# ScalarE's share of the gV blocks, and the pace of the weight gradients, in a decode block's forward and backward pass

## The chip, the cores and the metric

The kernel runs on one core of a Trainium2 chip. The metric is the device time of one execution in microseconds (us). The profile is one execution, taken by the hardware profiler. Engines: PE (TensorE), VectorE (DVE in the profile), ScalarE (ACT), GpSimd (POOL) and the issuing queue SyncE (SP). Each works off its own instructions in the order in which the program holds them.

## The reference

One decode step of a transformer block (2 sequences, 32 heads of 128, 4096 cached keys, width 640, all bfloat16) and its gradients by every input but one:

```python
h = x + A_ref(layernorm(x), k_cache, v_cache, wq, wo)   # scores, softmax, p @ v, then @ wo
h2 = h + B_ref(layernorm(h), w1, w2)                    # relu MLP, hidden width 1728
# returned: h2, and the gradients of x, k_cache, v_cache, wq, wo, w1, w2 for grad_out
```

For the attention the two large gradients are outer products, for each batch b and head h: the gradient of V is `p` (4096) times `go` (128), and that of K is `p * (go.v - dot) * scale` (4096) times `q` (128). Each is a 1 MB tensor, and there are 64 of either kind. The gradients of the four weight matrices are outer products too, of rank 2 (one term for each sequence).

## The kernel before

Each cached tile of 4096 x 128 lies in SBUF as [128, 32, 128]: 32 blocks (`NSC`) of 128 rows.

**First pass** (`p1_iter`, one head each): K is transposed on PE, the scores and the softmax are made, the products that later steps need are kept. Its 66 steps go over both batches.

**Second pass** (`p2_iter(j)` and `p2_tail(j)`, one turn j for each of 64 heads in the order `turns`): V comes in again (tile `W`, loaded on SyncE's queue; 12 of the 64 are kept from the first pass). PE transposes it in four groups (`pair_transpose`, L435; ScalarE copies each group out of PSUM, L440), and multiplies it by `go` (`pair_matvec`, L448). `rb` (L872, ScalarE) holds the rows `go` and `q` spread over all partitions; `pp` (L874, GpSimd) holds p, each value twice. Then VectorE makes the gradient of V, `gV`, in two halves of 16 blocks (`outer_half`, L832), and GpSimd's queue stores it (L900). In the next turn `p2_tail` makes `gsp` (L843) and from it the gradient of K, `gK`, in two halves on VectorE (L832), stored at L851. gV and gK take buffers of the group "g", five and later seven of them, W those of "ld", the weight gradients those of "f".

With `by_act`, ScalarE makes the last 8 blocks (`NSB`) of gV instead of VectorE, each as one copy of the row scaled by a column of `pf` (L899); `pf` is a float copy by GpSimd (L877). VectorE's second half is then 8 blocks instead of 16. Before the change this holds for the turns 14 to 31: those after the end of the first pass and below 32.

**Order.** A list `plan` pairs the steps of the first pass with turns of the second: from step 41 on every other step has a turn, and from turn 14 on there are turns alone. A turn is a Python generator; after each of its seven parts the loop calls `bg_step` for three queues of background work. Each queue earns a `rate` of credit for a part and takes the next piece when it has some. Queue 0 is the middle of the network and the `go` rows (`go_group`, VectorE dot products at L658). Queue 1 is `fin_gen`, the weight gradients: `rows_of` prepares rows (L913, L918, L920), `outer_rows` makes 152 outer products on PE (L950), copies each by ScalarE to a tile `ot` (L956), and stores it with 19 transfers issued on ScalarE's queue (L959). Queue 2 is `gx_gen`, the gradient of x (dot products at L658). Queues 1 and 2 begin when the pool `fin` is made, during turn 23; their rates are `RATE2` and `RATE3`.

The outcome of all this is one fixed order of instructions for each engine; nothing is decided on the chip.

Of the kernel before, what the change touches and what calls it, by code (L numbers as in the profile page):

```python
# [10 lines left out]
ACT = mybir.ActivationFunctionType  # L11
# [4 lines left out]
def kernel(  # L16
# [20 lines left out]
    nc = tc.nc  # L37

    B, Sq, D = A_x.shape
    _, H, Sk, Dh = A_k_cache.shape  # L40
# [4 lines left out]
    NSC = Sk // 128  # L45
# [7 lines left out]
    HALF = NSC // 2  # L53
# [153 lines left out]
    P_bf = cols.tile([128, NPS, NSC], BF16)  # L207
# [194 lines left out]
    NP1 = len(pairs)  # L402
# [6 lines left out]
    p_slot = {bh: n for n, bh in enumerate(pairs[:NPS])}  # L409
# [417 lines left out]
    def pairs_view(t):  # L827
        return t.rearrange("p s (a two) -> p s a two", two=2)

    def outer_half(dst, row, colp, k, n=HALF):  # L830
        sl = slice(k * HALF, k * HALF + n)
        nc.vector.tensor_tensor(  # L832
            out=pairs_view(dst[:, sl, :]),
            in0=row.rearrange("p (a two) -> p a two", two=2)[:, None, :, :].to_broadcast([128, n, 64, 2]),
            in1=colp[:, sl, None, :].to_broadcast([128, n, 64, 2]), op=ALU.mult)

    def p2_tail(j):

        p = S2[j]
        bp, hp = turns[j]  # L840
        pair_matvec(p["dp"], p.pop("T3"), 3, gom[:, bp, hp, :, :])
        gsp = small.tile([128, NSC, 2], BF16, tag="gsp", bufs=2, name="gsp")
        nc.vector.scalar_tensor_tensor(  # L843
            out=gsp[:], in0=p["dp"][:, :, None].to_broadcast([128, NSC, 2]), scalar=negdot[:, hp, bp:bp + 1],
            in1=P_bf[:, p_slot[(bp, hp)], :, None].to_broadcast([128, NSC, 2]), op0=ALU.add, op1=ALU.mult)
        yield
        gK = take("g", [128, NSC, 128], "gK")
        outer_half(gK, p["rb"][:, 128:256], gsp, 0)
        yield
        outer_half(gK, p["rb"][:, 128:256], gsp, 1)  # L850
        nc.gpsimd.dma_start(out=natural(out_2, bp, hp), in_=gK[:])  # L851
        give(gK)
        del S2[j]
        yield

    NSB = 8

    def p2_iter(j, by_act):

        tail = p2_tail(j - 1) if j - 1 in S2 and "T3" in S2[j - 1] else iter(())  # L860
        c = S2[j]
        next(tail, None)
        b, h = turns[j]
        go = gom[:, b, h, :, :]
        bank = pst([128, 512], FP32, "sps", "dp_ps")
        for k, col in enumerate((goc, qsc)):
            nc.tensor.matmul(bank[:, 128 + k * 128:256 + k * 128],  # L867
                             lhsT=col[:, h, b:b + 1].to_broadcast([128, 128]), rhs=ident_bf[:],
                             start=True, stop=True)
        c["dp"] = bank[:, 0:NSC]  # L870
        rb = mats.tile([128, 256], BF16, tag="rb", bufs=3, name="rb")
        nc.scalar.activation(out=rb[:], in_=bank[:, 128:384], func=ACT.Copy, scale=rt[:, b, h:h + 1])  # L872
        pp = small.tile([128, NSC, 2], BF16, tag="pp", bufs=2, name="pp")
        nc.gpsimd.tensor_copy(out=pp[:], in_=P_bf[:, p_slot[(b, h)], :, None].to_broadcast([128, NSC, 2]))  # L874
        if by_act:
            pf = small.tile([128, NSB], FP32, tag="pf", bufs=2, name="pf")
            nc.gpsimd.tensor_copy(out=pf[:], in_=P_bf[:, p_slot[(b, h)], NSC - NSB:NSC])  # L877
        c.update(rb=rb, pp=pp)
        c["T0"] = pair_transpose(c["W"], 0)
        next(tail, None)  # L880
        yield
        for _ in tail:
            yield
        c["T1"] = pair_transpose(c["W"], 1)
        pair_matvec(c["dp"], c.pop("T0"), 0, go)
        yield
        c["T2"] = pair_transpose(c["W"], 2)
        pair_matvec(c["dp"], c.pop("T1"), 1, go)
        yield
        c["T3"] = pair_transpose(c["W"], 3)  # L890
        give(c["W"], "g" if j < H and j != 1 and owned["g"] < 3 else None)
        pair_matvec(c["dp"], c.pop("T2"), 2, go)
        gV = take("g", [128, NSC, 128], "gV")
        outer_half(gV, c["rb"][:, 0:128], c["pp"], 0)
        yield
        outer_half(gV, c["rb"][:, 0:128], c["pp"], 1, HALF - NSB if by_act else HALF)
        if by_act:
            for k in range(NSB):
                nc.scalar.activation(out=gV[:, NSC - NSB + k, :], in_=rb[:, 0:128], func=ACT.Copy, scale=pf[:, k:k + 1])  # L899
        nc.gpsimd.dma_start(out=natural(out_3, b, h), in_=gV[:])  # L900
        give(gV)
        yield
# [190 lines left out]
    M0_ITERS = 7  # L1093
    P2_AT = H + 2 + M0_ITERS
    RATES = (0.2, 0.8, 0.2, 0.8, 0.45)
    RATE2 = 0.65
    RATE3 = 0.45
    plan = []
    i = j = 0
# [46 lines left out]
    fin = big1 = big2 = big3 = None  # L1146
    g2 = None
# [12 lines left out]
    for n, (i, j) in enumerate(plan):  # L1160
        all_go = all(("go", B - 1, h) in done for h in range(H))
        if i is None and plan[n - 1][0] is not None:
            pkp.release()
            big1 = tc.alloc_tile_pool(name="big1", bufs=1)
            for _ in range(2):
                more_home("ld", big1)
            share(ld=KEPT[1] + 4, g=5)
        if all_go and not late[0]:
            wop.release()
            big3 = tc.alloc_tile_pool(name="big3", bufs=1, side="right")  # L1170
            for tag in ("ld", "g", "g", "q", "q", "q"):
                more_home(tag, big3)
        late[0] = all_go
        more = int(late[0])
        if fin is not None and not bg2 and not bg3:
            share(ld=8 + 3 * more, g=7 + 3 * more)
        elif fin is not None and j >= H:
            held = sum(bh in kept for bh in turns[j + 1:])
            share(ld=5 + held + more, g=5 + 2 * more, f=3, q=2 + 3 * more)
        while g2 is not None:  # L1180
            p2_step()
        open_tail = [k for k in S2 if "T3" in S2[k]]
        if j is not None:
            if j < NP1:
                bg_until(("go", *turns[j]))
            g2 = p2_iter(j, i is None and j < H) if j < NP1 else p2_tail(NP1 - 1)
        elif open_tail:
            g2 = p2_tail(open_tail[0])
        if i is None and ("w1", 1) in done and fin is None:
            wts.release()  # L1190
            fin = tc.alloc_tile_pool(name="fin", bufs=1)
            big2 = tc.alloc_tile_pool(name="big2", bufs=1)
            more_home("f", big2)
            banks.update(sps=[2, 3], o=[4, 5, 6])
            bg2.append(("fin", fin_gen(fin)))
            bg3.append(("gx", gx_gen(fin)))
        if i == 12:
            bg.append(("ga", ga_gen()))
        if i == H + 2:
            banks["bc"].insert(0, banks["sps"].pop(0))  # L1200
        elif i == P2_AT:
            banks["bc"].remove(7)
            banks["sps"].insert(0, banks["bc"][0])
            banks["bc"] = [7]
        rate = RATES[0 if i is not None and i <= H + 1 else 1 if j is None and i < P2_AT else
                     2 if i is not None else 3 if j <= H else 4]
        if i is None:
            spread[0] = 2
            at_k[0] = 1
            k = 0  # L1210
            while g2 is not None:
                p2_step()
                pump()
                slot[0] = int(k in ((1, 3, 5) if j <= H else (1, 4)))
                k += 1
                bg_step(0, rate)
                bg_step(1, RATE2 * (0.4 if spreading[0] else 1.0))
                bg_step(2, RATE3)
            continue
        at = LIGHT if j is None else HEAVY_TAIL if open_tail else HEAVY  # L1220
        for k, _ in enumerate(p1_iter(i, i < H + 1, 0)):
            for _ in range(at.get(k, 0)):
                if g2 is not None:
                    p2_step()
            if k == 5:
                a_heads(i)
            pump()

            spread[0] = 1 if i < P2_AT else 2
            at_k[0] = k  # L1230
            if i >= P2_AT:
                slot[0] = int(k == 6 or (k == 1 and j is None))
            elif i > H + 1:
                slot[0] = {1: 2, 3: 1, 4: 1, 6: 1}.get(k, 0)
            else:
                slot[0] = int(k in (1, 6))
            bg_step(0, rate)
            bg_step(1, 0.0)
        if i is not None and i in (H + 1, NP1 + 1):
            bg.append((f"m{i // H - 1}", middle_gen(i // H - 1)))  # L1240
# [41 lines left out]
```

## Time and profile before

| | us |
|---|---|
| median of 3 runs (lowest, highest) | 897.04 (895.9, 898.17) |
| the profiled execution | 896.38 |
| its span, first to last instruction | 894.5 |
| busy: PE / VectorE / ScalarE / GpSimd | 744.0 / 684.9 / 483.4 / 196.1 |
| bytes moved | 361.84 MB, 405 GB/s in the mean |

In the profile a line such as `L899 ACT ACTIVATE gV<-rb,pf x144` names the line of the kernel, the engine, the operation, what is written from what, and the count. "DMA share" is the mean busy share of the 16 DMA engines. PEclk is the granted clock of TensorE as a share of full speed; its mean is 0.768, and in the second pass it is mostly 0.5.

### The profile page before, as it was taken

The page shows a single profiled execution, that of the slowest core. Times are in us where ns is not written, and L with a number is a line of the kernel's source. Part 1 is how long each engine was busy: PE and PEld are TensorE (multiplying, and loading weights), DVE is VectorE, ACT ScalarE, POOL GpSimd, SP SyncE. Part 2 cuts the span into 40 slices and gives each one's busy share as a digit, 9 for nine tenths or more (in the row PEclk, how much of TensorE's full clock was granted, in tenths as well). Part 3 has the DMA queues.
Part 4 walks back from the last instruction along what each step waited for, and adds up shares of the span by engine and source line. Part 5 has one row for each costly group of instructions (what it writes and reads, how often), then busy time and mean ns, then how long its engine had stood idle before and what let it go on. Part 6 is the DMA issues. An engine that isn't in the chain of part 4 may idle for free.

```text
span 894.5 us, 24705 instructions
## 1 busy us (share of the span) xinstructions
PE 744.0 (83%) x10145; PEld 619.9 (69%) x10145; DVE 684.9 (77%) x1283; ACT 483.4 (54%) x1236; POOL 196.1 (22%) x347
## 2 busy tenths in 40 slices
PE   4998899998998998798768786788798897988593
PEld 4887788888787887787657675567566665664453
DVE  2665788966888897697678896679886679978854
ACT  1443344443555665465446777776665765656462
POOL 1344434442210000000011231122221111111211
PEclk9999999999999999899895555555755756555555
DMA  9999999999989999999999999999999999999996
GB/s 376 419 411 404 409 407 419 410 414 410 364 299 374 421 423 424 424 420 424 406 374 399 416 418 421 385 417 389 421 421 411 422 425 425 425 425 426 423 407 271
DMA packets 56304, 361.84 MB, mean 405 GB/s; under 512 B 5696, under 2 KB 11904, under 8 KB 15488
## 3 DMA queue, kind: packets, MB, share of 16 engines
q1 hardware_dynamic: 34536, 211.13, 58.0%
q0 software_dynamic: 18432, 134.23, 36.1%
q10 hardware_dynamic: 3224, 14.92, 4.2%
q8 instruction: 80, 1.31, 0.6%
q14 instruction: 32, 0.26, 0.1%
HBM read 211.11 MB, written 149.13 MB: 403 GB/s over the span
## 4 chain that ended last, share of the span: by engine, by line
PE 40%; DMA 28%; DVE 17%; ACT 7%; issue 5%; SPq 0%; POOL 0%; ACTq 0%; POOLq 0%; DVEq 0%
PE t_ps L435 17%; DMA Vt<-in_A_v_cache_dram 12%; DMA out_dram<-gK 9%; PE m_ps L469 8%; DMA out_dram<-gV 5%; DVE gK L832 4%; DVE rows L658 4%; PE s_ps L448 3%; DVE gV L832 3%; DVE pk L476 3%; PE o_ps L950 3%; PE dp_ps L448 2%; ACT gV L899 2%; ACT t_sb L440 2%; PE u_ps L498 2%
## 5 line engine op out<-in xcount | busy, mean ns | idle before, releaser
L440 ACT COPY t_sb<-t_ps 128x512 f32<-128x512 f32 x479 | 271.9, 586 | 188.0 <-PE t_ps L435 184.5
L448 PEld LDWEIGHTS <-t_sb 128*128 128x128 bf16 x4096 | 169.8, 103 | 87.9 <-issue 39.8
L435 PE MATMUL t_ps<-ident_f,Wt 128*128 128x128 f32 x832 | 203.8, 398 | 0.7 <-ACT t_sb L440 0.7
L476 DVE TENSOR_TENSOR pk<-Kt,ep 128x2048 bf16<-128x2048 bf16 x128 | 156.2, 1221 | 42.5 <-ACT ep L523 23.4
L469 PE MATMUL m_ps<-pk,Vt 128*128 128x129 bf16 x2048 | 174.7, 223 | 16.7 <-DMA Vt<-in_A_v_cache_dram 15.4
L832 DVE TENSOR_TENSOR gK<-rb,gsp 128x2048 bf16<-128x2048 bf16 x128 | 153.0, 1223 | 15.1 <-DMA out_dram<-gV 13.3
L435 PEld LDWEIGHTS t_ps<-ident_f,Wt 128*128 128x128 f32 x832 | 142.4, 207 | 31.6 <-issue 23.6
L435 PE MATMUL t_ps<-ident_f,Kt 128*128 128x128 f32 x1024 | 149.7, 281 | 6.1 <-DMA Kt<-in_A_k_cache_dram 5.6
L832 DVE TENSOR_TENSOR gV<-rb,pp 128x2048 bf16<-128x2048 bf16 (+1 forms) x128 | 143.4, 1144 | 10.0 <-DMA out_dram<-gK 9.1
L469 PEld LDWEIGHTS <-Vt 128*128 128x128 bf16 x2048 | 129.9, 99 | 20.3 <-DMA Vt<-in_A_v_cache_dram 18.3
L435 PEld LDWEIGHTS t_ps<-ident_f,Kt 128*128 128x128 f32 x1024 | 113.3, 145 | 7.6 <-issue 4.9
L486 POOL COPY pk<-ep 128x16 bf16<-128x16 bf16 x80 | 83.0, 1039 | 151.6 <-ACT ep L523 111.9
L448 PE MATMUL dp_ps<-gom,t_sb 128*128 128x2 bf16 x2048 | 96.4, 168 | 19.0 <-ACT t_sb L440 18.5
L900 POOL DMA_DIRECT2D out_dram<-gV x64 | 34.2, 534 | 312.6 <-DVE nb L516 115.1
L448 PE MATMUL s_ps<-gom,t_sb 128*128 128x2 bf16 x2048 | 79.9, 164 | 1.5 <-DVE t_sb L438 1.5
L851 POOL DMA_DIRECT2D out_dram<-gK x64 | 34.0, 531 | 215.1 <-DVE gK L832 166.5
L582 ACT CAST MT<-m_ps 128x128 bf16<-128x128 f32 x64 | 17.0, 265 | 115.8 <-PE m_ps L469 115.8
L956 ACT CAST ot<-o_ps 128x512 bf16<-128x512 f32 (+3 forms) x152 | 67.6, 492 | 3.5 <-PE o_ps L950 1.9
L872 ACT ACTIVATE rb<-dp_ps,rt 128x256 bf16<-128x256 f32 x64 | 30.2, 471 | 42.4 <-PE dp_ps L867 41.2
L658 DVE CUSTOM_DVE_ANT_0 rows<-wo_t,rows 128x640 bf16<-128x640 bf16 x64 | 52.5, 820 | 0.2
L843 DVE SCALAR_TENSOR_TENSOR gsp<-dp_ps,negdot,P_bf 128x64 bf16<-128x64 f32 x64 | 17.9, 279 | 43.7 <-PE dp_ps L448 43.4
L658 DVE CUSTOM_DVE_ANT_0 rows<-wqs,gqr 128x1024 bf16<-128x1024 bf16 x40 | 48.8, 1219 | 0.2
(194 smaller groups left out, 759.5 us busy)
## 6 DMA issues: line engine op xcount, KB each, us to landing
Kt<-in_A_k_cache_dram SPq DMA_DIRECT2D x64, 1024.0 KB, 16.8
Vt<-in_A_v_cache_dram SPq DMA_DIRECT2D x64, 1024.0 KB, 17.0
out_dram<-gV POOLq DMA_DIRECT2D x64, 1024.0 KB, 12.2
out_dram<-gK POOLq DMA_DIRECT2D x64, 1024.0 KB, 12.9
Wt<-in_A_v_cache_dram SPq DMA_DIRECT2D x52, 1024.0 KB, 12.8
out_dram<-ot ACTq DMA_DIRECT2D x6, 960.0 KB, 8.6
wq_t<-in_A_wq_dram SPq DMA_DIRECT2D x5, 1024.0 KB, 7.0
wqs<-in_A_wq_dram SPq DMA_DIRECT2D x5, 1024.0 KB, 21.9
```

The lines of the kernel that those rows point to most:

```text
L435: nc.tensor.transpose(t_ps[:, j, :], natf[:, 2 * cc:2 * cc + 2, :].rearrange("p c k -> p (c k)"), ident_f[:])
L440: nc.scalar.copy(out=t_sb[:], in_=t_ps[:])
L448: nc.tensor.matmul(dst[:, sc:sc + 2], lhsT=v[:, j, :, par], rhs=vecs[:, par, :], start=(par == 0), stop=(par == 1))
L469: nc.tensor.matmul(r["m"][:, 0:129], lhsT=r["V"][:, sc, :], rhs=r["pk"][sc // HALF][:, sc % HALF, 0:129], start=(sc == 0), stop=(sc == NSC ...
L476: nc.vector.tensor_tensor(out=p["pk"][k][:, :, 0:128].rearrange("p s (a two) -> p s a two", two=2), in0=p["K"][:, sl, :].rearrange("p s (a ...
L486: nc.gpsimd.tensor_copy(out=col, in_=e)
L658: nc.vector.tensor_tensor_reduce(out=junk[0:kc, 0:width], in0=in0, in1=in1, scale=1.0, scalar=0.0, op0=ALU.mult, op1=ALU.add, accum_out=acc)
L832: nc.vector.tensor_tensor(out=pairs_view(dst[:, sl, :]), in0=row.rearrange("p (a two) -> p a two", two=2)[:, None, :, :].to_broadcast([128 ...
L851: nc.gpsimd.dma_start(out=natural(out_2, bp, hp), in_=gK[:])
L872: nc.scalar.activation(out=rb[:], in_=bank[:, 128:384], func=ACT.Copy, scale=rt[:, b, h:h + 1])
L900: nc.gpsimd.dma_start(out=natural(out_3, b, h), in_=gV[:])
L956: nc.scalar.copy(out=ot[0:P, k, n0:n0 + nn], in_=o_ps[0:P, 0:nn])
```

## The change

The argument of `p2_iter` becomes a number of blocks, `nsb`, in place of a flag. Turns 14 to 23 keep 8 blocks on ScalarE, as long as `fin` does not exist; turns 24 to 31 have none, so VectorE makes their whole gV; the last three turns, 61 to 63, which had none, get 4. `RATE2` goes from 0.65 to 0.7, so that the pieces of `fin_gen` come earlier in the order: its last piece stands in turn 59 instead of turn 62.

```diff
-    def p2_iter(j, by_act):
+    def p2_iter(j, nsb):
...
-        if by_act:
+        if nsb:
             pf = small.tile([128, NSB], FP32, tag="pf", bufs=2, name="pf")
-            nc.gpsimd.tensor_copy(out=pf[:], in_=P_bf[:, p_slot[(b, h)], NSC - NSB:NSC])
+            nc.gpsimd.tensor_copy(out=pf[:, 0:nsb], in_=P_bf[:, p_slot[(b, h)], NSC - nsb:NSC])
...
-        outer_half(gV, c["rb"][:, 0:128], c["pp"], 1, HALF - NSB if by_act else HALF)
-        if by_act:
-            for k in range(NSB):
-                nc.scalar.activation(out=gV[:, NSC - NSB + k, :], in_=rb[:, 0:128], func=ACT.Copy, scale=pf[:, k:k + 1])
+        outer_half(gV, c["rb"][:, 0:128], c["pp"], 1, HALF - nsb)
+        if nsb:
+            for k in range(nsb):
+                nc.scalar.activation(out=gV[:, NSC - nsb + k, :], in_=rb[:, 0:128], func=ACT.Copy, scale=pf[:, k:k + 1])
...
-    RATE2 = 0.65
+    RATE2 = 0.7
...
-            g2 = p2_iter(j, i is None and j < H) if j < NP1 else p2_tail(NP1 - 1)
+            nsb = 0 if i is not None else NSB if j < H and fin is None else NSB // 2 if j >= NP1 - 3 else 0
+            g2 = p2_iter(j, nsb) if j < NP1 else p2_tail(NP1 - 1)
```

## The prediction

> A **turn** below is one head of one batch in the second pass, numbered as in `turns` (0 to 63); turns 14 to 63 run after the first pass has ended, and the ScalarE instruction `rb` (L872) marks where each starts. Times are positions in the profiled execution.
>
> **What bounds the kernel now.** I read the page's 40 slices first, then busy times by stretch, then the line that the change touches, the chain that ended last, and the last turns in order of time.
>
> ```profile
> DMA  9999999999989999999999999999999999999996
> GB/s 376 419 411 404 409 407 419 410 414 410 364 299 374 421 423 424 424 420 424 406 374 399 416 418 421 385 417 389 421 421 411 422 425 425 425 425 426 423 407 271
> ```
>
> The transfers are the limit: their share is at its ceiling nearly everywhere, and 361.84 MB over the span is 404 GB/s against the 424 to 426 of the best slices. All bytes are the same after the change, so time can be won only where a slice is below that rate. In the second pass these are slices 26 and 28 (385 and 389) and the last two. By stretch:
>
> ```profile
> core 0: us, PE busy (x) PEld busy (x) DVE busy (x) ACT busy (x) POOL busy (x), PEclk, DMA share, GB/s
> 541.73:612.61 70.88, 54.12 (x483) 42.79 (x482) 52.70 (x98) 51.52 (x143) 14.92 (x32) 0.52 1.00 406
> 612.61:623.00 10.39, 9.05 (x97) 7.73 (x97) 10.32 (x16) 6.14 (x14) 3.15 (x6) 0.50 1.01 374
> 690.00:760.00 70.00, 58.89 (x581) 43.68 (x579) 52.51 (x68) 44.20 (x96) 10.56 (x23) 0.62 1.01 424
> 760.00:830.00 70.00, 58.21 (x462) 40.34 (x461) 60.70 (x87) 43.07 (x95) 10.27 (x21) 0.52 1.01 425
> 860.00:894.50 34.50, 18.82 (x158) 13.62 (x156) 17.39 (x18) 13.34 (x25) 4.21 (x9) 0.50 0.77 315
> ```
>
> The first row holds turns 24 to 31, the ones that lose their ScalarE blocks: no engine is full (VectorE 74%, ScalarE 73%), the rate is 406. There the engines wait for each other in a ring. The line moved by the change, and the chain in this stretch:
>
> ```profile
> L899 ACT ACTIVATE gV<-rb,pf x144: 384/389/414, 476.6 to 612.3; 128x128 bf16<-128x128 bf16 x144
>   POOL out_dram L900: 57.1, 12
> ```
>
> ```profile
> 567.27 2.44 ACT gV L899 x8
> 571.03 0.87 PE t_ps L435 x4
> ...
> 578.28 2.45 ACT gV L899 x8
> ```
>
> Eight blocks take 3.1 us of ScalarE after a turn's last copy out of PSUM. The copies of the weight gradients and the next `rb` queue behind them, and PE waits for both. The pieces of L899 on the chain from 541.73 to 612.61 sum to 13.4 us (2.44, 1.85, 2.44, 2.45, 1.67, 0.68, 1.85). From 690 to 830 the transfers run full, so faster engines win nothing there. The last row is the tail: no loads are left, and the stores wait for turns.
>
> ```profile
> 870.90 0.47 ACT L872 ACTIVATE rb<-dp_ps,rt 128x256 bf16<-128x256 f32 x1 [0.72 <-PE dp_ps L867]
> ...
> 875.75 0.59 ACT L440 COPY t_sb<-t_ps 128x512 f32<-128x512 f32 x1 [0.93 <-PE t_ps L435]
> 877.03 0.47 ACT L872 ACTIVATE rb<-dp_ps,rt 128x256 bf16<-128x256 f32 x1 [0.70 <-PE dp_ps L867]
> 877.88 0.59 ACT L440 COPY t_sb<-t_ps 128x512 f32<-128x512 f32 x1 [0.38 <-PE t_ps L435]
> ...
> 881.09 0.58 ACT L440 COPY t_sb<-t_ps 128x512 f32<-128x512 f32 x1 [0.56 <-PE t_ps L435]
> ```
>
> ScalarE has gaps of 0.4 to 0.9 us; each copy waits for PE. The turns from 59 on start at 843.28, 850.87, 860.27, 870.90 and 877.03.
>
> **The change part by part.** The profiled execution took 896.38 us, 1.88 of it outside its span of 894.5; the median of the runs is 897.04, 0.66 above. I sum changes and put them on the median.
>
> *Turns 24 to 31, whole gV on VectorE.* The `fin` pool is made during turn 23, so 8 turns lose 8 blocks: 64 x 0.389 = 24.9 us of ScalarE less. VectorE's second half is 128x2048 (1.22 us) instead of 128x1024 (0.68): 8 x 0.54 = 4.3 us more, on an engine with 70.88 - 52.70 = 18.2 us idle there. GpSimd loses 5 `pf` copies of 0.2 to 1.2 us in all (18 become 13). For the chain: 13.4 less at best, 4.3 more at worst, so 9 us of engine time. The transfers cap it: 70.88 x (1 - 406/424.5) = 3.1 us is all that a full rate can win. The cover of VectorE's 4.3 us is its idle time; without it they are on the path. Bounds -3.1 to +4.3; I take -2.0, near the first end because idle time is four times the addition, and short of it because the rate dips also in rows where the share is 1.00. What is late next is then the transfers.
>
> *RATE2 0.65 to 0.7.* The same 152 outer products (PE about 0.6, a ScalarE copy 0.59) and 19 stores on ScalarE's queue, each earlier. In the order of the program, the last product leaves turns 60 and 61 (8 each before, and two trailing copies in 62) and all are done in turn 59; turn 58 gets nine, turn 59 eight copies instead of four. A product's price in the tail: turn 60 took 9.40 us and 61 10.63, where 62, almost without them, took 6.13; so 0.41 to 0.56, say 0.49. Turn 58 (14.85 us) has VectorE busy for 13.43 and PE for 6.55, so nine more products lie beside VectorE's work; uncovered they would cost 4.4. Turn 59: +1.9. Turn 60: -3.3. Turn 61: -4.5. Sum -5.9 us of engine time. In turns 24 to 57 the same products only move by up to two turns, through a stretch whose transfers are full.
>
> *Four blocks by ScalarE in turns 61 to 63.* 12 x 0.389 = 4.7 us of ScalarE; VectorE's second half is 128x1536, which no row shows: between 0.68 and 1.22, I take 0.95, 0.27 less. That wins nothing: VectorE waits for PE before `gsp` in each of the last turns. ScalarE pays: turn 62's last copy ends at 876.34, four blocks take it to 877.9, so `rb` slips from 877.03 and the copy behind it ends 0.5 us later. PE's matvecs wait for that copy. Two turns (62 and 63) at 0 to 1.56 us; I take 0.5 each, from those gaps. The last gV also waits: 881.67 + 1.56 = 883.2, so its store goes out about 1.5 us later than 882.04. The last gK, issued at 885.12, still ends the kernel; its data may find gV's in front of it, 0 to 1.0 us.
>
> *What the tail can give.* Engines: -5.9 + 1.0 = -4.9, bounds -5.9 to -1.8. Transfers: 34.5 us at 315 GB/s are 10.9 MB, 25.6 us at 424.5, so 8.9 idle. From the last issue to the end (885.12 to 894.5) are 9.4 us of which some 1.6 MB need 3.8, so 5.6 stay. At most 3.3 can go. I take -2.2, a third off for the last gV and for weight-gradient stores no longer there to fill gaps. Sum: -2.0 - 2.2 = -4.2, and 897.04 - 4.2 = 892.8.
>
> **Rivals.** About 0.3% (2.7 us, so 894.35 and 899.73) is what a measurement here can tell from no change.
>
> *Only one recovery, or neither.* The stores only change places: what weight gradients no longer use at the end, the turns, pushed back by 1 to 2 MB (2.4 to 4.9 us of transfers), take. For it: share 1.01 over 623 to 860 means that bytes moved forward push others back. Against: turn 58 is held by VectorE, so it hides that. Gain 0 to 2.5, say 895.5.
>
> *Slower: VectorE paces turns 24 to 31.* From 612.61 to 623.00 VectorE is 99% busy and the rate is 374. If 4.3 us more put the eight turns there too, their 28.8 MB at 374 would take 77.0 us, +6.1; with the tail's -2.2 this is 900.9. It decides once VectorE nears 99%; the sum gives (52.70 + 4.3)/70.88 = 80%. Turns 28 and 31 are already at 99%, but each follows one with room.
>
> *GpSimd behind VectorE.* GpSimd's `pp` copy takes 257 ns in the median and 1211 at most, the long ones beside VectorE's products; its store issues stay at 531 to 534 ns. If each of the eight gV stores went out 0.54 us later for VectorE's longer half, and nothing took that up, the stretch would lose 4.3 instead of winning 2.0: 897.04 + 4.3 - 2.2 = 899.1. Against: the issues keep their length, and the copies have a whole turn of room. The Trainium skill (SBUF — State Buffer, "Who interferes with whom") says that a VectorE instruction with two SBUF inputs and a GpSimd instruction that reads SBUF exclude each other for a whole instruction, which speaks against handing blocks to VectorE. By that rule, the trace agrees for the copies, and shows nothing of it in the store issues.
>
> *The tail's blocks cost in full.* 2 x 1.56 + 1.0 = 4.1 eats the tail's share: 897.04 - 2.0 + 0.8 = 895.8, no difference.
>
> **Numbers.** The forecast, with its variants up to both caps in full (897.04 - 3.1 - 3.3 = 890.6) and a little beyond: 0.60, all faster. One recovery or neither 0.19, the tail's blocks in full 0.06, GpSimd behind VectorE 0.03: together 0.28, within 0.3%. VectorE's pace 0.12, slower. The forecast's own range is 890 to 894.3; with the cases in between 889.5 to 899, which leaves out VectorE's pace and the little above or below.
>
> **What would show it.** Right: the stretch of turns 24 to 31 shorter by about 2 us with a rate above 410; no L899 between 545 and 840; turns 60 and 61 near 6.1 us; idle transfer time in the last 34.5 us down from 8.9 to 6 or 7. Wrong: VectorE above 95% in turns 24 to 31; turns 62 and 63 over 7 us because `rb` stands behind gV blocks; the rate after 623 below 418; or turn 58 over 16 us.

## The result, and the profile after

| | before | after |
|---|---|---|
| median of 22 runs each (lowest, highest), us | 897.5 (895.9, 901.78) | 900.63 (894.86, 903.23) |
| ratio to before, 95% interval | | 1.003 (1.0017 to 1.0042) |
| the profiled execution, its span, us | 896.38, 894.5 | 899.5, 897.7 |

The change makes the kernel slower by 0.3%. The forecast was 892.8, with a range of 889.5 to 899: both the direction and the range were wrong.

The slices of the page show where. After:

```profile
DMA  9999999999879999999999999999999999999997
GB/s 378 419 410 404 410 407 419 410 413 411 346 292 376 421 423 423 423 422 423 405 392 402 417 419 415 418 421 419 389 386 336 409 424 424 425 424 425 426 422 294
```

Slices 25 to 28 are at 415 to 421, where before had dips to 385 and 389: won, as forecast. But three new dips (389, 386, 336) stand in slices 29 to 31, which before has at 421, 421 and 411. By stretch, after:

```profile
core 0: us, PE busy (x) PEld busy (x) DVE busy (x) ACT busy (x) POOL busy (x), PEclk, DMA share, GB/s
542.60:602.00 59.40, 52.06 (x477) 40.90 (x477) 50.70 (x88) 34.27 (x78) 10.37 (x24) 0.50 1.01 418
640.00:700.00 60.00, 51.55 (x409) 37.21 (x408) 43.55 (x74) 36.33 (x80) 9.13 (x21) 0.50 0.94 361
700.00:860.00 160.00, 125.50 (x1159) 91.03 (x1157) 133.53 (x188) 100.45 (x216) 26.14 (x51) 0.59 1.01 424
860.00:897.70 37.70, 16.85 (x193) 14.77 (x191) 20.38 (x22) 14.07 (x32) 9.41 (x15) 0.59 0.83 346
```

The second row of these in the kernel before:

```profile
640.00:700.00 60.00, 51.49 (x471) 38.94 (x470) 46.83 (x78) 39.51 (x83) 12.54 (x24) 0.57 1.01 416
```

Turns 24 to 31 (first row) take 59.4 us instead of 70.88, at 418 GB/s instead of 406. The 60 us from 640 run at 361 instead of 416, and VectorE, which makes what is stored, is less busy in them. I turn rates into lost transfer time as the prediction did, us x (1 - rate/424.5):

| lost transfer time, us | 0-540 | 540-620 | 620-640 | 640-700 | 700-860 | 860-end | sum |
|---|---|---|---|---|---|---|---|
| before | 27.8 | 4.4 | 0.1 | 1.2 | 0.2 | 8.9 | 42.7 |
| after | 27.9 | 1.2 | 0.2 | 9.0 | 0.2 | 7.0 | 45.4 |

The stretch gains 3.2, the tail 1.9, and 640 to 700 loses 7.8: 2.7 net. All bytes are the same, so the rest of the 3.2 by which the span grew is rounding of the rates. What the head start turns into stands on the chain of after, from 586 to 632 (start, us, what):

```profile
586.34 18.67 DMA out_dram<-gK
...
605.13 2.37 DVE gV L832 x2
...
607.79 17.90 DMA out_dram<-gV
...
625.77 2.40 DVE gK L832 x2
```

The turns run into their own stores: VectorE waits for a buffer whose store takes 18 us. Turn 32 starts 10.6 us earlier than before (602.0 against 612.6), but turn 35 only 1.1 earlier (632.7 against 633.8). From there the turns are longer than before, and the queue of stores gets short. Issues from 640 to 700, with the median time to landing at the end, before and then after:

```profile
out_dram<-gV POOLq DMA_DIRECT2D x8, 1024.0 KB, 14.2
out_dram<-gK POOLq DMA_DIRECT2D x8, 1024.0 KB, 14.4
```

```profile
out_dram<-gK POOLq DMA_DIRECT2D x7, 1024.0 KB, 6.6
out_dram<-gV POOLq DMA_DIRECT2D x7, 1024.0 KB, 8.1
```

Two stores fewer are issued, and a store lands in half the time, since fewer stand in front of it: 16 stores of 14.3 us in 60 us are about 3.8 under way at a time, 14 of 7.4 us about 1.7. The DMA share falls from 1.01 to 0.94, which is about half of the lost rate. For the other half the transfer engines count as busy and move less (340 GB/s at a share of 0.99 from 670 to 680); no run shows why. The lengths of the turns, from `rb` to `rb`, with the outer products that the program puts into each in brackets:

| turn | before | after |
|---|---|---|
| 35 | 4.65 (0) | 7.51 (0) |
| 36 | 5.55 (1) | 9.12 (6) |
| 37 | 7.93 (7) | 9.77 (8) |
| 38 | 7.90 (8) | 9.26 (6) |
| 39 | 8.97 (4) | 7.63 (0) |
| 60, 61, 62 | 9.40 (8), 10.63 (8), 6.13 (0) | 4.80, 5.76, 4.92 (0 each) |

### The profile page after: what moved, and what is told of

It reads as the page before. It is cut to its first block, busy times and chain, and to the rows that moved or that the text cites. A ratio compares the mean times of both kernels' runs of the same rounds, so it can differ in the third digit from the quotient of the medians.

```text
span 897.7 us, 24636 instructions
## 1 busy us (share of the span) xinstructions
PE 741.6 (83%) x10145; PEld 621.1 (69%) x10145; DVE 689.1 (77%) x1283; ACT 470.1 (52%) x1184; POOL 192.4 (21%) x342
## 4 chain that ended last, share of the span: by engine, by line
DMA 35%; PE 35%; DVE 16%; ACT 7%; issue 5%; SPq 0%; POOL 0%; ACTq 0%; POOLq 0%; DVEq 0%
PE t_ps L435 16%; DMA Vt<-in_A_v_cache_dram 13%; DMA out_dram<-gV 7%; DMA out_dram<-gK 6%; DMA Kt<-in_A_k_cache_dram 6%; PE m_ps L469 6%; DVE gK L832 4%; DVE rows L658 4%; DVE gV L832 3%; DVE pk L476 3%; DMA wqs<-in_A_wq_dram 3%; ACT t_sb L440 3%; PE s_ps L448 3%; PE o_ps L950 2%; PE dp_ps L448 2%
## 5 line engine op out<-in xcount | busy, mean ns | idle before, releaser
L435 PE MATMUL t_ps<-ident_f,Wt 128*128 128x128 f32 x832 | 201.0, 393 | 0.7 <-ACT t_sb L440 0.7
L469 PE MATMUL m_ps<-pk,Vt 128*128 128x129 bf16 x2048 | 175.5, 223 | 15.3 <-DMA Vt<-in_A_v_cache_dram 14.6
L435 PEld LDWEIGHTS t_ps<-ident_f,Wt 128*128 128x128 f32 x832 | 139.9, 204 | 32.9 <-issue 25.8
L832 DVE TENSOR_TENSOR gV<-rb,pp 128x2048 bf16<-128x2048 bf16 (+2 forms) x128 | 146.9, 1172 | 14.3 <-DMA out_dram<-gK 10.2
L435 PE MATMUL t_ps<-ident_f,Kt 128*128 128x128 f32 x1024 | 151.9, 284 | 4.4 <-DMA Kt<-in_A_k_cache_dram 4.2
L658 DVE CUSTOM_DVE_ANT_0 rows<-w_t,rows 128x640 bf16<-128x640 bf16 (+2 forms) x58 | 46.0, 793 | 3.5 <-ACT rows L636 2.8
```

The costliest lines, as they stand in the source:

```text
L435: nc.tensor.transpose(t_ps[:, j, :], natf[:, 2 * cc:2 * cc + 2, :].rearrange("p c k -> p (c k)"), ident_f[:])
L469: nc.tensor.matmul(r["m"][:, 0:129], lhsT=r["V"][:, sc, :], rhs=r["pk"][sc // HALF][:, sc % HALF, 0:129], start=(sc == 0), stop=(sc == NSC ...
L658: nc.vector.tensor_tensor_reduce(out=junk[0:kc, 0:width], in0=in0, in1=in1, scale=1.0, scalar=0.0, op0=ALU.mult, op1=ALU.add, accum_out=acc)
L832: nc.vector.tensor_tensor(out=pairs_view(dst[:, sl, :]), in0=row.rearrange("p (a two) -> p a two", two=2)[:, None, :, :].to_broadcast([128 ...
```

## The experiments

Each ran beside the kernel before on the same chip; ratios are to it, with 95% intervals.

**The parts alone.** Each of the three parts was run alone, and the first two together.

```diff
# only_blocks (against the change): part 1 alone
-            nsb = 0 if i is not None else NSB if j < H and fin is None else NSB // 2 if j >= NP1 - 3 else 0
+            nsb = 0 if i is not None else NSB if j < H and fin is None else 0
-    RATE2 = 0.7
+    RATE2 = 0.65
# only_rate: part 2 alone (RATE2 = 0.7)
+            nsb = 0 if i is not None else NSB if j < H else 0
# only_tail: part 3 alone (RATE2 = 0.65)
+            nsb = 0 if i is not None else NSB if j < H else NSB // 2 if j >= NP1 - 3 else 0
# no_tail: parts 1 and 2 (RATE2 = 0.7)
+            nsb = 0 if i is not None else NSB if j < H and fin is None else 0
```

> One part alone: turns 24 to 31 have their whole gV made by VectorE; RATE2 stays 0.65, and the last three turns have no ScalarE blocks. Theory 1 (running ahead): this part alone lets turns 24 to 31 finish about 10 us sooner; the turns then meet full store buffers near 605 to 625, PE pauses, keeps half clock through turns 34 to 38, these take 7.5 us and more where they took 4.7 to 8, and the transfers run dry between 640 and 700. Expected: no gain or a loss, 897 to 900, with windows under 380 GB/s between 640 and 700. Theory 2 (weight gradients too early): this part is harmless, it only wins the 3 us that were forecast: 893 to 895, no dip.

> One part alone: RATE2 0.7, ScalarE blocks as before the change. Theory 1: the tail wins up to 2 to 3 us as forecast, nothing dries up at 640 to 700: 894 to 897. Theory 2: the products moved forward into turns 36 to 38 make these turns 9 us and more and dry up the transfers there: 898 to 901, with the dip, whatever makes gV in turns 24 to 31.

> One part alone: four blocks by ScalarE in turns 61 to 63, all else as before the change. Theories 1 and 2 both: 0 to +1 us (the rb instructions of turns 62 and 63 slip by about 0.5 us each). Theory 3 (the tail's blocks cost in full): +2.5 to +4 us.

> The change without its third part: whole gV on VectorE in turns 24 to 31 and RATE2 0.7, no ScalarE blocks in turns 61 to 63. Theories 1 and 2: as slow as the whole change, within 1 us (about 900), with the dip between 640 and 700. Theory 3: back to 896 or 897.

| | median, us | ratio | lost 640-700, us |
|---|---|---|---|
| only_blocks | 895.01 | 0.9983 (0.9972 to 0.9995) | 2.2 |
| only_rate | 898.81 | 1.0025 (1.0010 to 1.0039) | 5.2 |
| only_tail | 898.56 | 1.0015 (1.0005 to 1.0024) | 1.6 |
| no_tail | 899.57 | 1.0030 (1.0019 to 1.0041) | 9.0 |

Theory 1 fell: only_blocks wins, and its turns 35 to 38 are as short as before (4.9, 5.4, 7.9, 7.9), although it too runs ahead by 8.5 us at turn 32 and gives it back in 32 to 34. Theory 2 stands for the loss: with the rate alone turns 35 to 38 take 7.3, 8.3, 9.8 and 9.3. The profiled execution of only_rate was the fastest of its runs, so its 5.2 is rather a low value; its share in the row is 1.00, at 388 GB/s. no_tail loses another 3.2 us from 620 to 640, where the whole change loses 0.2. The rate costs about 1.8 us alone, and about 4.6 once part 1 is there (899.57 against 895.01). Row 640 to 700 of only_blocks:

```profile
640.00:700.00 60.00, 50.10 (x474) 37.38 (x474) 46.98 (x79) 39.60 (x85) 12.40 (x24) 0.63 1.01 409
```

The tail's blocks cost about 1.5 us alone (897.02 to 898.56), between theories 2 and 3. There they stand in the way of the weight gradients. Turn 61 of only_tail, ScalarE:

```profile
869.90 1.28 ACT L899 ACTIVATE gV<-rb,pf 128x128 bf16<-128x128 bf16 x4 [0.74 <-ACT ot L956]
871.09 1.04 ACT L956 CAST ot<-o_ps 128x512 bf16<-128x512 f32 x2
872.86 0.47 ACT L872 ACTIVATE rb<-dp_ps,rt 128x256 bf16<-128x256 f32 x1 [0.73 <-PE dp_ps L867]
```

Two copies out of PSUM queue behind four blocks, and the turn takes 12.0 us instead of 10.6. In the changed kernel no products are left there, and the whole change and no_tail have the same ratio, 1.003.

**Which turns the rate costs in.** Parts 1 and 2, with the rate changed at turn 44 (35 and 42 in the third):

```diff
# late_rate
-                bg_step(1, RATE2 * (0.4 if spreading[0] else 1.0))
+                bg_step(1, (0.65 if j < 44 else 0.75) * (0.4 if spreading[0] else 1.0))
# early_rate
+                bg_step(1, (0.7 if j < 44 else 0.6) * (0.4 if spreading[0] else 1.0))
# hold_rate
+                bg_step(1, (0.65 if j < 35 else 0.35 if j < 42 else 0.8) * (0.4 if spreading[0] else 1.0))
```

> As no_tail (whole gV on VectorE in turns 24 to 31, no blocks in turns 61 to 63), but the weight gradients' rate is 0.65 up to turn 43 and 0.75 from turn 44 on: turns 35 to 43 have the products that they had before the change (0, 1, 7, 8, 4 in turns 35 to 39), and the last product stands in turn 59 as after the change. Theory (the loss is made by products and row work moved into turns 35 to 38, where the transfers need short turns): transfer time lost from 640 to 700 about 2 us as in only_blocks, not 9; the tail keeps its gain; 893.5 to 895.5, faster than only_blocks by 0 to 1.5. Rival (ending three turns sooner costs by itself, wherever the products go): 898 to 900, as only_rate and no_tail.

> The opposite: as no_tail, but the rate is 0.7 up to turn 43 and 0.6 from turn 44 on: turns 35 to 39 have the products of the changed kernel (2, 6, 8, 6, 0), and the last product stands in turn 62 as before the change. Theory: 9 us of transfer time lost from 640 to 700 and the tail of before, 899 to 902. Rival: as only_blocks, 894 to 896.

> As no_tail, but the rate is 0.65 up to turn 34, 0.35 in turns 35 to 41 and 0.8 from turn 42 on: turns 35 to 41 have 0, 0, 2, 4, 4, 4 and 5 products, fewer than either kernel, and the last product stands in turn 61. Theory: if short turns from 35 to 41 are what the transfers need, the time lost from 640 to 700 falls to 1 or below: 893 to 895. If a turn of seven to eight products is no worse there than elsewhere, no different from late_rate.

| | median, us | ratio | lost 640-700, us | lost 860-end, us |
|---|---|---|---|---|
| late_rate | 897.13 | 0.9991 (0.9979 to 1.0004) | 1.9 | 9.9 |
| early_rate | 899.39 | 1.0019 (1.0005 to 1.0034) | 9.0 | 6.9 |
| hold_rate | 897.40 | 0.9988 (0.9975 to 1.0002) | 3.7 | 8.8 |

Row 640 to 700 of late_rate, then of early_rate:

```profile
640.00:700.00 60.00, 50.63 (x476) 37.61 (x475) 47.98 (x79) 39.64 (x85) 13.43 (x24) 0.62 1.01 411
```

```profile
640.00:700.00 60.00, 50.41 (x442) 35.94 (x441) 45.92 (x78) 37.41 (x85) 10.39 (x23) 0.59 0.95 361
```

The dip follows the rate up to turn 43 and not the end of the weight gradients: late_rate ends them in turn 59 like the change and has no dip; early_rate ends them in turn 62 like before and has it whole (and loses 2.3 more from 620 to 640). The stores issued from 640 to 700 land after 14.4 us in late_rate, and after 6.2 (gK) and 8.9 us (gV) in early_rate. That it is turns 35 to 42 which matter is read from the traces; no run changes them alone. The counts in two expectations are off: in early_rate, as in the change, turns 35 to 39 have 0, 6, 8, 6 and 0 products, and hold_rate's 0, 0, 2, 4, 4, 4 and 5 stand in turns 36 to 42.

Two expectations missed. late_rate isn't faster than only_blocks, though its turns 60 to 62 take 4.8, 5.4 and 4.9 us. And hold_rate loses 3.7 from 640 to 700 with still shorter turns (35 to 38 at 4.4, 4.1, 4.6 and 6.5). Of this, 2.2 fall into 640 to 656.5, the short turns themselves, which run at 360 and then 378 GB/s with shares of 0.97 and 0.99, while stores land after 12 us; in turn 39, which then takes 11.3 us, the rate is 415. So short turns alone don't keep the rate full, and why it is lower there stays open.

**Where late_rate's tail went.** The end of late_rate and of before, after the last engine's work:

```profile
886.00:893.00 7.00, 0.00 (x0) 0.00 (x0) 0.00 (x0) 0.00 (x0) 0.00 (x0) 0.50 0.06 26
```

```profile
888.00:893.00 5.00, 0.00 (x0) 0.00 (x0) 0.00 (x0) 0.00 (x0) 0.00 (x0) 0.50 0.24 98
```

A DMA share of 0.06 is one of 16 engines, and the trace has one packet under way at a time there. In late_rate the others are done by about 886, and one works on alone for nearly 7 us, although the last store was issued at 879.2, where before issued it at 885.1. The share and the rate up to then are means over 16, and say nothing of it. One more run ends the products another two turns earlier, and one had no ScalarE blocks at all:

```diff
# late85 (against late_rate)
+                bg_step(1, (0.65 if j < 44 else 0.85) * (0.4 if spreading[0] else 1.0))
# no_blocks (against only_blocks)
+            nsb = 0
```

> As late_rate, but the rate is 0.85 from turn 44 on, so the last product stands in turn 57 instead of 59. Theory (in the tail the mean share hides one transfer engine that has fallen behind while all were full; it works on alone at the end): the mean rate stays above 415 until the last stores, one engine runs on alone (share 0.06) for 5 us or more, and nothing is won: 896 to 898.5, as late_rate. Rival (the tail is still limited by the turns' engines, so fewer products there help): faster than late_rate by 1 us or more, 894 to 896.

> As only_blocks, but turns 14 to 23 too have their whole gV made by VectorE, so ScalarE makes none at all. In those turns VectorE is already 93% busy between 500 and 520, so here the rival that was predicted for turns 24 to 31 should come true: turns 17 to 22 go from 6.4 to about 6.9 us, VectorE near 99%, and the time from 463 to 542 grows by 3 to 5 us. If the transfers limit these turns as well, that is hidden: 894.5 to 896; if VectorE paces them it is not: 897 to 900.

late85: 896.81, ratio 0.9993 (0.9979 to 1.0006), in the theory's range: its turns 58 to 62 take 5.2, 5.0, 5.1, 5.0 and 3.9 us, its last `rb` stands at 867.9 (before: 877.0), and no gain can be told. But its trace bears the theory out only in part. At the end some five us pass with the share at 0.14 or less, where only_blocks has four; it loses 7.5 us from 860 on, less than late_rate, and 3.2 from 640 to 700. late_rate has the same order of instructions up to turn 43 and loses 1.9 there: by so much two executions can differ.

no_blocks: 896.22, ratio 0.9994 (0.9983 to 1.0006), so not told from before. My expectation missed: turns 17 to 21 got shorter, not longer (6.3, 7.2, 5.1, 4.2, 3.9 against 6.9, 8.1, 6.4, 6.4, 6.4), and turns 22 and 23 (9.8 and 17.7) gave all of it back. From 500 to 520, before and then no_blocks:

```profile
500.00:520.00 20.00, 16.96 (x164) 14.73 (x163) 18.59 (x32) 15.60 (x43) 4.96 (x11) 0.50 1.01 415
```

```profile
500.00:520.00 20.00, 16.93 (x236) 14.55 (x235) 16.76 (x27) 13.33 (x25) 3.14 (x7) 0.83 1.01 420
```

PE finished 236 instructions where before had 164, at a clock of 0.83 instead of 0.50, and VectorE was less busy, not more. So VectorE had been waiting in a ring with ScalarE's blocks, not pacing it.

**The version that beats both** is only_blocks, part 1 alone: 895.01, 0.9983 of before (0.9972 to 0.9995).

## Why the prediction was wrong, point by point

*Turns 24 to 31.* Right, and better than the -2.0 taken: 3.2 us of lost transfer time went, the cap of 3.1 in full. ScalarE's line after:

```profile
L899 ACT ACTIVATE gV<-rb,pf x92: 384/388/406, 476.8 to 880.5; 128x128 bf16<-128x128 bf16 x92
```

The engines won 11.5 us (70.88 to 59.40), against the 9 worked out. What I didn't see is that this was not kept: the turns wait in 32 to 34. Alone, in only_blocks, the part is worth about 2 us (ratio 0.9983), as taken.

*RATE2.* This is the step that failed. The prediction said of turns 24 to 57 that the products "only move by up to two turns, through a stretch whose transfers are full". I priced them by engine time in the tail and at nothing elsewhere, and took a DMA share of 1.01 for a cover. But what kept that share up were the turns themselves. Turns 35 and 36, at 4.65 and 5.55 us, put 2 MB of stores each into the queue, as much as the transfers carry in 4.9 us at 424.5 GB/s, and loads besides. In the change they take 7.5 and 9.1, and the queue of stores gets short. The cover was the queue's depth, which the landing times show (14 us before, 7 to 8 after); I had looked at landing times only over the whole kernel. Size: +7.8 us of lost transfer time from 640 to 700, against the 0 put down; late_rate and early_rate show that it comes with the rate up to turn 43.

Why the turns get longer: turn 36 has five products more, and the same work also falls at other places in the turns. Turn 35 has no product in either kernel and three `wide` copies (L913, for the rows of the weight gradients) in both, and yet takes 2.9 us more. Its start on PE, before and then after:

```profile
633.53 1.91 PE L435 MATMUL t_ps<-ident_f,Wt 128*128 128x128 f32 x8
...
635.50 0.59 PE L918 MATMUL rw_ps<-ident_bf,wide 128*128 128x128 bf16 x4
```

```profile
632.44 1.06 PE L435 MATMUL t_ps<-ident_f,Wt 128*128 128x128 f32 x4
634.30 0.61 PE L918 MATMUL rw_ps<-ident_bf,wide 128*128 128x128 bf16 x4 [0.80 <-ACT wide L913]
```

After, PE stands 0.80 us until ScalarE has made `wide`, and the next transposes stand behind that; before, eight transposes come first and there is no such wait. With products it is the same. Turn 38 before has PE run three of them at once, right after the first transpose:

```profile
651.61 1.06 PE L435 MATMUL t_ps<-ident_f,Vt 128*128 128x128 f32 x4
652.61 0.62 PE L950 MATMUL o_ps<-ghfr,x2r 2*128 2x512 bf16 x3
653.16 1.11 PE L435 MATMUL t_ps<-ident_f,Vt 128*128 128x128 f32 x4
```

Turn 37 after, also with eight:

```profile
649.13 1.06 PE L435 MATMUL t_ps<-ident_f,Wt 128*128 128x128 f32 x4
650.12 0.61 PE L950 MATMUL o_ps<-ghfr,x2r 2*128 2x512 bf16 x1
651.41 0.31 PE L950 MATMUL o_ps<-ghfr,x2r 2*128 2x192 bf16 x1 [0.67 <-ACT ot L956]
651.65 1.11 PE L435 MATMUL t_ps<-ident_f,Wt 128*128 128x128 f32 x4
```

There a product waits 0.67 us for a PSUM bank that ScalarE has still to copy, and the next transpose stands behind it. From transpose to transpose it is 2.5 us instead of 1.55. PE's clock may add something: 0.77 and 0.89 in turns 35 and 36 before, 0.50 after; but only_rate had 0.63 and 0.60 there and its turns were as long within 0.9 us, which speaks for the order; no run separates the two.

*The tail.* The engine sum was -4.9; turns 59 to 62 took 25.5 us instead of 33.75, -8.2. Of transfer time 1.9 was won, near the 2.2 taken. But in late_rate, with turns 59 to 62 as short and no dip before, the gain didn't reach the end: the rate from 860 to 880 is 417 instead of 366, and one transfer engine finishes late. That is one trace; late85 shows it less. "At most 3.3 can go" was worked out from a mean over 16 engines; the last engine is what ends the kernel. Turn 58 stayed at 14.6 us with the nine products, as predicted.

*Four blocks in turns 61 to 63.* "0.5 each" was right in kind:

```profile
873.76 0.58 ACT L440 COPY t_sb<-t_ps 128x512 f32<-128x512 f32 x1 [0.56 <-PE t_ps L435]
874.24 1.27 ACT L899 ACTIVATE gV<-rb,pf 128x128 bf16<-128x128 bf16 x4
875.42 0.46 ACT L872 ACTIVATE rb<-dp_ps,rt 128x256 bf16<-128x256 f32 x1
```

After, `rb` of turn 63 starts right behind the blocks; four take 1.27 us together, not 1.56. It costs nothing that can be told in the change, and 1.5 us alone.

*The rivals.* VectorE did not pace turns 24 to 31 (50.70 of 59.40 us, 85%), and no_blocks shows that it didn't where it was 93% busy either. That the measured 900.63 lies beside this rival's 900.9 is chance: the rival has the stretch 6.1 us longer, the run has it 11.5 shorter. GpSimd behind VectorE: the store issues of gV still take 534 ns in the mean, and only_blocks is faster; by that rule of the Trainium skill (SBUF — State Buffer, "Who interferes with whom") a loss was possible, and no run here shows one. The rival that came true in part was the first, "bytes moved forward push others back". It was given a gain of 0 to 2.5; that moving work could leave the transfers idle was not among the cases.

*The signs.* All four signs of being right came: the stretch is shorter, at 418 GB/s; no L899 stands between 545 and 840; turns 60 and 61 are below 6.1 us; 7.0 us are lost from 860 on. Of the signs of being wrong one came, the rate after 623 below 418: it is 361 from 640 to 700.

*What stays open.* Why the rate costs 1.8 us alone and about 4.6 with part 1 is argued from the store queue (turns 32 to 34 wait with it, and it is shorter when the long turns come), but no run separates it. Why the rate falls by more than the share, there and in hold_rate, isn't shown. And which transfer engine falls behind, and by what, is not in these traces.

## What to carry to other kernels

A queue that is always busy is not cover for work placed in front of it: look at how deep it is in that stretch (the time from issue to landing) and at which turns fill it, and price moved work turn by turn along the whole way that it moves, not only where it leaves. Run the parts of a compound change one by one: here one part won 0.17%, the other two lost 0.25% and 0.15%. A mean over 16 transfer engines can't tell when the last one is done.

## What the runs showed that I had not expected

In late_rate the transfers' mean share is 1.01 from 860 to 880, and yet one of 16 engines ends nearly 7 us after the others (share 0.06 from 886 to 893). In before, whose transfers had dipped shortly ahead of the end, the last part at a share of 0.12 or less is about 3 us, in after 4. A share near 1 is not a full rate either: after has 340 GB/s at 0.99 from 670 to 680, and only_rate 388 at 1.00 from 640 to 700. Taking ScalarE's blocks away let PE run at a clock of 0.83 instead of 0.50 from 500 to 520, where only what ScalarE, VectorE and GpSimd (`pf`) do for gV had been changed.
